# Attention in small steps for one more batch element, and Newton steps dealt out between products

## The chip, the cores and the metric

The kernel runs on one core of one Trainium2 chip. The metric is device time in microseconds (us). Before the change the median of three runs is 1347.16 us (1345.57 to 1347.76).

## The reference

Attention with RMS-normalised queries and keys, then one mixer layer over tokens and channels, in fp32 for q, k, v and with float64 weights:

```python
# q, k, v: (8, 12, 448, 64)
q_n, k_n = rmsnorm(q, g_q), rmsnorm(k, g_k)
attn = softmax(q_n @ k_n.T / sqrt(64))
x = (attn @ v).transpose(0, 2, 1, 3).reshape(8, 448, 768)
# token mixing: w_tok1 (448, 256), w_tok2 (256, 448)
u = x + (relu(x.T @ w_tok1) @ w_tok2).T
# channel mixing: w_ch1 (768, 1536), w_ch2 (1536, 768)
out = u + relu(u @ w_ch1) @ w_ch2
```

## The kernel before

**Work and its order.** The eight batch elements pass one after the other through the mixer. While element b is in the mixer, the attention of batch b + 1 is computed (AHEAD = 1) between the mixer's products. TensorE, VectorE, ScalarE and GpSimd run their instructions in the order in which the code issues them; only SyncE's DMA queue is ordered by the framework's scheduler.

**Attention.** Two heads are a pair, six pairs (NPAIR) a batch. Two pairs (four heads) are one t, so t runs from 0 to 23, three per batch. The 448 keys of a t are seven key blocks k of 64. `score(t, k)` makes 4 matmuls of 64x64 tiles into two s_ps tiles and two exponentials into an e tile; `values` multiplies e with v into o_ps; `group_sums` adds the e tiles of a t into es (k = 1, 2 on POOL, the rest on DVE); `row_sums` multiplies es by ones into d_ps. `denominators` for two pairs are two parts begin (a transpose and a reciprocal, which free d_ps) and two parts end (a transpose and a product, which free o_ps). There are four s_ps tiles (shared with d_ps), two o_ps and two m_ps tiles (for the mixer's products), four e tiles, and from t = BIG on a fifth e tile in cv_sb.

**Preparing the next t.** While t is computed, its successor's pairs n and n + 1 are prepared: `loads` (eight DMAs a pair from batch 2 on, into one of two qk_t slots), `square` on ACT, `reduce` on DVE, `roots`, `scale` on DVE, `turn_qk` (transposes). `roots` is a fold (four ACT copies, L1282), a guess (DVE, L1291 and L1296) and three Newton steps of three DVE instructions each (L1315 to L1317) on 128x56 elements.

**Small steps and large blocks.** Up to batch 1, attention comes in small steps, `att_step(g)` with g = 4t + s: four steps a t, with one or two key blocks of scores and of values each. Their items carry costs, and `merge` mixes them with the mixer's items in proportion to cost. From t = BIG on there are two large blocks a t (`big_step`): the first holds scores 0, 1 and 2 and the last values and row sums of t - 1; the second holds scores 3 to 6 and values 0 to 3. `place` puts six blocks per element ahead of the channel products number 0, 6, 11, 17, 22 and 28 (BLOCKS). A block's list `ahead` goes before it, `beside` directly behind it, and `between` is dealt out evenly over the products up to the next block.

**The mixer.** Token products (`tok1`, `tok2`, L754 and L762), then channel products in a seven-product form: 21 for `ch1` (L878), 21 for `ch2` (L935), each of 128x224 matmuls with weights from 384 KB unit loads, evicted by DVE (hb L883 and others), ACT or POOL. Element 0 instead multiplies with the weights as they are converted (`first_stage`, L850), with the conversion on DVE and ACT at the same time; in element 1, POOL also makes the weight sums (raw L204, loaded and stored by DMA, `sums`).

**Around the change.** In element 0 the attention list is the steps of batch 1 and, at its end, the first block of t = 6. In element 1, blocks 2 of t = 6 to 1 of t = 9 are placed. `cv_sb` serves the conversion in element 0.

Of the kernel before, what the change touches and what calls it, by code (L numbers as in the profile page):

```python
# [44 lines left out]
def whole(ctx, tc, shifted, pre, q, k, v, g_q, g_k, moe_w_tok1, moe_w_tok2, moe_w_ch1, moe_w_ch2, out):  # L45
# [6 lines left out]
    B, H, S, D = q.shape  # L52
# [6 lines left out]
    NPAIR = H // 2  # L59
# [50 lines left out]
    st = dict(pre.st)  # L110
# [262 lines left out]
    def e_tile(spare=False):  # L373

        if spare:
            return cv_sb[:].rearrange("p i n -> p (i n)")[:, 0:2 * S].rearrange("p (i s) -> p i s", i=2)
        return e_pool.tile([P, 2, S], F32, name="e")

    def score(t, k):

        e = st["e", t, k] = e_tile(t >= BIG and ((t - BIG) * NK + k) % 5 == 4)
        pss = [s_tile("s_ps") for i in range(2)]
        for i in range(2):
            qkT = st["qkT", 2 * t + i]
            for a in range(2):
                h = slice(a * D, a * D + D)
                nc.tensor.matmul(  # L387
                    out=pss[i][rows_of(i, a), 0:S], lhsT=qkT[h, 1, k * D:(k + 1) * D], rhs=qkT[h, 0, :],
                    start=True, stop=True)
        for i in range(2):  # L390
            nc.scalar.activation(out=e[:, i, :], in_=pss[i][:, 0:S], func=AF.Exp)  # L391
# [77 lines left out]
    def row_sums(t):  # L469
        es = st.pop(("es", t))  # L470
        for p in (2 * t, 2 * t + 1):
            st["d", p] = s_tile("d_ps")
            ones(p, es[:, p % 2, :], start=True, stop=True)

    def denominators(ps):

        def begin(p):
            b, j = divmod(p, NPAIR)
            if j == 0:
                st["uT", b] = uT_pool.tile([P, NC, S], F32, name="uT")  # L480
            ps = st.pop(("d", p))

            dt = rd_pool.tile([P, S], F32, name="dt", tag="rd")
            if shifted:
                nc.vector.tensor_scalar(dt[:], ps[:, 0:S], 1e-9, None, ALU.add)
                src = dt[:]
            else:

                src = ps[:, 0:S]
            nc.vector.transpose(out=dt[:], in_=src)  # L490
            st["rc", p] = rc = pre.nt_pool.tile([P, NB], F32, name="rc")
            nc.vector.reciprocal(out=rc[:], in_=dt[:].rearrange("p (n c) -> p n c", c=32)[:, :, 0])

        def raw(p):

            b, j = divmod(p, NPAIR)
            to = st["uT", b][:, j, :]
            nc.scalar.copy(out=to, in_=st["o", p][:, 0:S])
            st["o", p] = to

        def end(p):
            b, j = divmod(p, NPAIR)
            rd = rd_pool.tile([P, S], F32, name="rd", tag="rd")
            nc.vector.transpose(
                out=rd[:].rearrange("p (n c) -> p n c", c=32),
                in_=st.pop(("rc", p))[:].unsqueeze(2).to_broadcast([P, NB, 32]))
            nc.vector.tensor_tensor(out=st["uT", b][:, j, :], in0=st.pop(("o", p))[:, 0:S], in1=rd[:], op=ALU.mult)

        parts = [lambda p=p: begin(p) for p in ps]
        if ps[0] < NPAIR:  # L510
            parts += [lambda p=p: raw(p) for p in ps]
        return parts + [lambda p=p: end(p) for p in ps]

    NG = 2 * NP
    BIG = NPAIR

    def big_step(t, second):

        p, n = 2 * t, 2 * t + 2
        pair, last, live, more = (p, p + 1), (p - 2, p - 1), p < NP, 2 * t + 2 < NP  # L520
        item = lambda fn, *a, c=0.4: (c, lambda: fn(*a))
        loads = lambda j: [(0.3, fn) for fn in pre.loads(j, st, nc.sync, nc.sync)] if j < NP else []

        def first_block():
            if live:
                score(t, 0)
                score(t, 1)
            if more:
                pre.reduce(n, st)
                pre.square(n + 1, st)  # L530
            for k in range(NK - 2 - (t > BIG), NK):
                values(last, k)
            row_sums(t - 1)
            for i in last:
                st.pop(("v", i))
            if live:
                score(t, 2)

        def second_block():
            score(t, 3)  # L540
            score(t, 4)
            for k in range(4):
                values(pair, k)
            score(t, 5)
            score(t, 6)
            for i in pair:
                st.pop(("qkT", i))

        if not second:
            ahead = [item(pre.square, n, st)] if more else []  # L550
            beside = [item(pre.reduce, n + 1, st)] + [(0.4, fn) for fn in pre.roots(n, st)] if more else []
            between = [(0.4, fn) for fn in denominators(last)]
            between += [item(load_v, i, c=0.0) for i in pair if live]
            between += [item(group_sums, t, k) for k in (1, 2) if live]
            return ahead, (5.4, first_block), beside, between
        beside = [item(scale, n), item(scale, n + 1), item(turn_qk, n, 1), item(turn_qk, n, 0)] if more else []
        beside += [item(group_sums, t, k) for k in (3, 4)]
        between = [item(turn_qk, n + 1, 1), item(turn_qk, n + 1, 0)] + loads(n + 2) if more else []
        between += [item(group_sums, t, k) for k in (5, 6)] + loads(n + 3)
        return [], (6.2, second_block), beside, between  # L560
# [20 lines left out]
    def att_step(g):  # L581
# [101 lines left out]
        if not inside:  # L683
            items += part(turns)
        if g == 4 * BIG - 1 and not shifted:
            items += part(pre.loads(n + 3, st, nc.sync, nc.sync), 0.3)
# [294 lines left out]
    def y_order(b):  # L981

        return [o * KC + m for m in ((0, 1, 2) if b else (2, 0, 1)) for o in range(2)]

    def sends(b, cs):
        return [(0.3, lambda cc=cc: send_y(b, cc, st.pop(("y", cc)))) for cc in cs]
# [3 lines left out]
    def x_items(b, h):  # L990
        return [(0.1, lambda j=j: trans_x(b, j)) for j in range(h * NC // 2, (h + 1) * NC // 2)]

    def tok1_items(b, h):
        return [(us(NS, HC), lambda j=j, h=h: tok1(b, j, h)) for j in range(NJ)]
# [15 lines left out]
    def in_next(b):  # L1010


        return b < B - 1 and not shifted
# [36 lines left out]
    AHEAD = 1  # L1050
# [35 lines left out]
    per = NPAIR * 2  # L1086
# [8 lines left out]
    att_items = lambda lo, hi: [it for g in range(lo, hi) for it in att_step(g)]  # L1095
# [4 lines left out]
    for b in range(B):  # L1100
        early, double = middle_items(b)
        if b == 0:
            early, last = first_items(
                tok1_items(0, 0) + x_items(0, 1) + tok1_items(0, 1) + early, double, some)
        else:
            if b > 1 and in_next(b - 1):

                y, z = sends(b - 1, y_order(b - 1)[:4]), left
                left = [y[0], y[1], z[0], y[2], z[1], y[3]]
            run(merge(tok1_items(b, 0), left[:2]))  # L1110
            begin, early = merge(tok1_items(b, 1) + early[:3 * KC], left[2:]), early[3 * KC:]
            if b == 1:
                early, double = merge(begin + early, sums[5:20]), merge(double, sums[20:])
                begin = []
            early = begin + early + double
            early, last = early[:-4], early[-4:]
        lo = (b + AHEAD) * per + 1
        att = []
        if b + AHEAD < B and (shifted or not b):
            att = att_items(lo, lo + 10) + x_items(b + AHEAD, 0) + att_items(lo + 10, lo + per - (b == 0 and not shifted))  # L1120
            if not shifted:
                ahead, block, beside, between = big_step(BIG, False)
                att += ahead + [block] + beside + between
        elif b + AHEAD < B:
            t = (b + AHEAD) * NPAIR // 2
            blocks = [big_step(t + i // 2, i % 2) for i in range(1, NPAIR + 1)]
            blocks[4][3].extend(x_items(b + 1, 0))
            early = place(early, blocks, [near(early, at) for at in BLOCKS])
        if b == 0:
            last = x_items(1, 1) + merge(last, direct + sums[:5], turns(b, y_order(b)[2:4]))  # L1130
        else:
            if b + 1 < B:
                last = merge(last, x_items(b + 1, 1))
            last += last_items(b)
        run(merge(att, early) + last)
        if b == 0:
            load_units(0)
        left = turns(b, y_order(b)[4:])
# [187 lines left out]
def kernel(  # L1326
# [33 lines left out]
    with arm.Else():  # L1360
        whole(tc, True, pre, *args)
# [30 lines left out]
```

## Time and profile before

| | |
|---|---|
| median of 3 runs | 1347.16 us |
| the profiled execution, own time | 1349.28 us |
| its span (first to last instruction) | 1347.5 us |
| PE busy | 1276.4 us (95%) |
| DVE, POOL, ACT busy | 748.0, 383.1, 370.5 us |
| mean granted TensorE clock | 0.982 |
| element 1, from its first token product to the next one's | 176.4 us |
| elements 2 to 5, the same | 153.6 to 153.8 us each |

Everything in the profile is one execution. A line of the timeline gives the start, the length, the engine, the code line, the operation, the tile written and those read, shapes, how many instructions, and in brackets the idle time of that engine before it with what ended it. The window rows give busy time by engine, the granted clock and DMA's share for a stretch of the span.

### The profile page before, as it was taken

How to read it: one execution, taken by the hardware profiler on the slowest of the kernel's cores; microseconds unless marked ns; L12 is line 12 of the kernel's file. 1: busy time of each engine (PE TensorE's matmuls, PEld its weight loads, DVE VectorE, ACT ScalarE, POOL GpSimd, SP SyncE). 2: the span in 40 equal slices, each digit the busy share in tenths (PEclk: the TensorE clock that was granted, in tenths of full speed). 3: DMA queues.
4: the chain of work that ended last, by engine and by line, in shares of the span. 5: the costliest groups of instructions: out<-in, count | busy, mean ns of one | idle time of the engine just before them, and what ended most of it. 6: DMA issues, size and time to landing. Idle time of an engine off the chain costs nothing.

```text
span 1347.5 us, 20173 instructions
## 1 busy us (share of the span) xinstructions
PE 1276.4 (95%) x7408; PEld 937.7 (70%) x7408; DVE 748.0 (56%) x1289; ACT 370.5 (27%) x740; POOL 383.1 (28%) x449
## 2 busy tenths in 40 slices
PE   5989998899699999999999999999999999999997
PEld 3444444346578867786787867786777967797996
DVE  6887759824565256654566356654566456433212
ACT  5553423302332033311333033311343023300100
POOL 1211522164465123321223123322223213311220
PEclk9999998889899999999999999999999999999998
DMA  9655477789778867585766866585766954486554
GB/s 211 164 161 158 120 179 210 179 201 252 208 213 193 209 136 177 139 224 107 173 153 154 218 136 149 138 221 122 174 150 149 231 122 129 120 210 139 177 172 93
DMA packets 502448, 228.05 MB, mean 169 GB/s; under 512 B 374532, under 2 KB 464004, under 8 KB 502340
## 3 DMA queue, kind: packets, MB, share of 16 engines
q1 hardware_dynamic: 489218, 224.83, 67.7%
q10 hardware_dynamic: 12994, 1.84, 0.8%
q8 instruction: 61, 1.00, 0.3%
q14 instruction: 47, 0.39, 0.1%
q0 software_dynamic: 128, 0.00, 0.0%
HBM read 187.07 MB, written 39.52 MB: 168 GB/s over the span
## 4 chain that ended last, share of the span: by engine, by line
PE 69%; DVE 3%; DMA 3%; ACT 2%; POOL 1%; SPq 1%; issue 1%; ACTq 0%; DVEq 0%; POOLq 0%
PE m_ps L935 25%; PE m_ps L878 20%; PE s_ps L387 7%; PE o_ps L461 7%; PE m_ps L754 5%; PE m_ps L762 5%; PE d_ps L441 1%; ACT half L1282 1%; DMA qk_t<-in_k_dram 1%; DVE nt L1316 1%; DVE nt L1315 1%; DVE rs L1317 1%; DVE hb L908 0%; DMA ws<-raw 0%; ACT e L391 0%
## 5 line engine op out<-in xcount | busy, mean ns | idle before, releaser
L935 PEld LDWEIGHTS m_ps<-hb,unit 128*128 128x128 f32 x1764 | 332.5, 190 | 8.7 <-issue 8.5
L935 PE MATMUL m_ps<-hb,unit 128*128 128x224 f32 x1764 | 338.0, 353 | 0.0
L878 PE MATMUL m_ps<-tu,unit 128*128 128x224 f32 x1008 | 201.4, 354 | 0.0
L878 PEld LDWEIGHTS m_ps<-tu,unit 128*128 128x128 f32 x1008 | 189.2, 190 | 13.0 <-issue 5.6
L391 ACT ACTIVATE e<-s_ps 128x448 f32<-128x448 f32 x286 | 134.5, 549 | 213.5 <-PE s_ps L387 213.5
L878 PE MATMUL m_ps<-uT,unit 128*128 128x224 f32 x756 | 156.5, 361 | 23.7 <-DVE hb L883 19.1
L878 PEld LDWEIGHTS m_ps<-uT,unit 128*128 128x128 f32 x756 | 144.6, 194 | 32.8 <-DVE hb L883 21.2
L387 PE MATMUL s_ps<-qkT 64*64 64x448 f32 x1260 | 145.3, 548 | 4.2 <-ACT x L734 4.1
L461 PE MATMUL o_ps<-e,v 64*64 64x448 f32 x1116 | 129.2, 545 | 0.1
L944 POOL TENSOR_TENSOR uT<-uT,r 128x448 f32<-128x448 f32 (+1 forms) x56 | 49.6, 896 | 236.6 <-DVE r L944 151.1
L883 DVE TENSOR_TENSOR r<-m_ps,r 128x448 f32<-128x448 f32 x63 | 39.3, 623 | 111.9 <-PE m_ps L878 58.5
L944 DVE TENSOR_TENSOR uT<-uT,m_ps 128x448 f32<-128x448 f32 (+1 forms) x70 | 34.0, 502 | 119.6 <-PE m_ps L935 119.6
L387 PEld LDWEIGHTS s_ps<-qkT 64*64 64x64 f32 x1260 | 45.9, 133 | 72.9 <-issue 58.5
L429 DVE TENSOR_TENSOR es<-es,e 128x896 f32<-128x896 f32 x70 | 83.3, 1190 | 21.1 <-POOL es L429 16.5
L883 POOL TENSOR_TENSOR hb<-r,r 128x448 f32<-128x448 f32 x21 | 23.8, 1133 | 245.7 <-ACT r L899 236.6
L754 PE MATMUL m_ps<-x,w_sb 112*128 112x384 f32 x256 | 87.5, 500 | 4.2 <-DMA x<-xs 3.2
L461 PEld LDWEIGHTS o_ps<-e,v 64*64 64x64 f32 x1116 | 45.6, 135 | 62.3 <-issue 59.0
L1274 DVE TENSOR_REDUCE ms<-sq 128x28 f32<-128x896 f32 (+2 forms) x45 | 48.7, 1083 | 52.6 <-ACT sq L1260 50.0
L884 ACT ACTIVATE hb<-hb 128x448 f32<-128x448 f32 x63 | 36.3, 577 | 148.8 <-DVE hb L883 128.2
L754 PEld LDWEIGHTS m_ps<-x,w_sb 112*128 112x128 f32 x256 | 49.6, 195 | 39.6 <-issue 7.8
L762 PE MATMUL m_ps<-w_sb,h 128*128 128x448 f32 x192 | 74.7, 543 | 0.0
L767 DVE TENSOR_TENSOR uT<-uT,m_ps 128x448 f32<-128x448 f32 x48 | 29.4, 614 | 65.3 <-PE m_ps L762 65.3
(124 smaller groups left out, 1438.9 us busy)
## 6 DMA issues: line engine op xcount, KB each, us to landing
unit<-ws SPq DMA_DIRECT2D x294, 384.0 KB, 3.9
raw<-in_moe_w_ch_dram SPq DMA_DIRECT2D x72, 256.0 KB, 3.5
v<-in_v_dram SPq DMA_DIRECT2D x96, 112.0 KB, 3.7
xs<-xt SPq DMA_DIRECT2D x56, 168.0 KB, 4.3
x<-xs SPq DMA_DIRECT2D x14, 672.0 KB, 6.5
out_dram<-turned SPq DMA_DIRECT2D x168, 56.0 KB, 1.9
qk_t<-in_q_dram SPq DMA_DIRECT2D x144, 56.0 KB, 3.4
qk_t<-in_k_dram SPq DMA_DIRECT2D x144, 56.0 KB, 3.7
```

The lines of the kernel that those rows point to most:

```text
L387: nc.tensor.matmul(out=pss[i][rows_of(i, a), 0:S], lhsT=qkT[h, 1, k * D:(k + 1) * D], rhs=qkT[h, 0, :], start=True, stop=True)
L391: nc.scalar.activation(out=e[:, i, :], in_=pss[i][:, 0:S], func=AF.Exp)
L429: eng.tensor_tensor(out=es[:], in0=(es if k > 1 else st["e", t, 0])[:], in1=st["e", t, k][:], op=ALU.add)
L461: nc.tensor.matmul(out=st["o", p][a * D:(a + 1) * D, 0:S], lhsT=vt[rows, k * D:(k + 1) * D], rhs=e[rows, :], **kw)
L754: nc.tensor.matmul(out=ps[:, 0:HC], lhsT=w1_sb[0:R, c, jc * P:(jc + 1) * P], rhs=st["x", b, h][0:R, :, c, :], start=(c == 0), stop=(c == N ...
L762: nc.tensor.matmul(out=ps[:, 0:S], lhsT=st["h1", jc][:, cc * P:(cc + 1) * P], rhs=w2_sb[:, jc].rearrange("p c r -> p (c r)"), start=(jc == ...
L878: nc.tensor.matmul(out=ps[:, j * HS:(j + 1) * HS], lhsT=w[:, t, j, :], rhs=m, start=(t == 0), stop=(t == KC - 1))
L883: add = lambda e, o, x, y: e.tensor_tensor(out=o, in0=x, in1=y, op=ALU.add)
L884: relu = lambda x: nc.scalar.activation(out=x, in_=x, func=AF.Relu)
L935: nc.tensor.matmul(out=ps[:, j * HS:(j + 1) * HS], lhsT=st["w"](j, t), rhs=hb[:, HB[what], t, :], start=(t == 0), stop=(t == KF - 1))
L944: add = lambda e, o, x, y: e.tensor_tensor(out=o, in0=x, in1=y, op=ALU.add)
L1274: self.nc.vector.tensor_reduce(out=st["ms", p][:, p % 2, lo:hi], in_=sq[:, lo:hi], axis=AX_X, op=ALU.add)
```

## The change

BIG becomes NPAIR + NPAIR // 2 = 9 instead of 6. So the attention of batch 2 comes in small steps too: the last item in element 0 is step g = 24 (scores 0 of t = 6) instead of a first block, and element 1 merges steps 25 to 35 and then the first block of t = 9 with its mixer items, from the second half of the first token product on. Elements 2 to 6 place their blocks as before. The fifth e tile is used from t = 9 on.

In every first block's lists, `roots` leaves `beside` and goes to `between`. The order of `between` becomes: the group sums 1 and 2, the fold, both begins, the guess, then end, Newton step, end, Newton step, the last Newton step, and the two loads of v.

```diff
-    BIG = NPAIR
+    BIG = NPAIR + NPAIR // 2
...
         if not second:
             ahead = [item(pre.square, n, st)] if more else []
-            beside = [item(pre.reduce, n + 1, st)] + [(0.4, fn) for fn in pre.roots(n, st)] if more else []
-            between = [(0.4, fn) for fn in denominators(last)]
-            between += [item(load_v, i, c=0.0) for i in pair if live]
-            between += [item(group_sums, t, k) for k in (1, 2) if live]
+            beside = [item(pre.reduce, n + 1, st)] if more else []
+            between = [item(group_sums, t, k) for k in (1, 2) if live]
+            ends, roots = ([(0.4, fn) for fn in fns] for fns in (denominators(last), pre.roots(n, st) if more else []))
+            between += roots[:1] + ends[:2] + roots[1:2]
+            between += [it for both in zip(ends[2:], roots[2:4]) for it in both] if more else ends[2:]
+            between += roots[4:] + [item(load_v, i, c=0.0) for i in pair if live]
             return ahead, (5.4, first_block), beside, between
...
-        if b + AHEAD < B and (shifted or not b):
-            att = att_items(lo, lo + 10) + x_items(b + AHEAD, 0) + att_items(lo + 10, lo + per - (b == 0 and not shifted))
-            if not shifted:
+        if b + AHEAD < B and (shifted or b < 2):
+            att = att_items(lo, lo + 10) + x_items(b + AHEAD, 0) + att_items(lo + 10, lo + per - (b == 1 and not shifted))
+            if b and not shifted:
                 ahead, block, beside, between = big_step(BIG, False)
                 att += ahead + [block] + beside + between
```

## The prediction

> **What bounds the kernel now.** I read the page first. PE is busy for 95% of the span and its row of slices is nearly solid, so only PE's idle time and its slow stretches can be taken out; the clock row dips in the first third alone.
>
> ```profile
> PE 1276.4 (95%) x7408; PEld 937.7 (70%) x7408; DVE 748.0 (56%) x1289; ACT 370.5 (27%) x740; POOL 383.1 (28%) x449
> PEclk9999998889899999999999999999999999999998
> ```
>
> Next the busy time by stages. The cuts are the times at which an element's first token product (L754) starts; the columns are window, length, then busy us of PE, PEld, DVE, ACT, POOL, then clock, DMA share and GB/s.
>
> ```profile
> 127.00:284.60 157.60, 147.98 (x580) 69.09 (x573) 116.10 (x189) 49.67 (x94) 53.54 (x78) 0.96 0.68 171
> 284.60:461.00 176.40, 160.09 (x925) 123.84 (x924) 86.80 (x152) 42.49 (x88) 82.23 (x122) 0.94 0.87 224
> 614.80:768.60 153.80, 151.44 (x922) 118.44 (x921) 85.86 (x152) 42.25 (x87) 40.87 (x32) 1.00 0.69 162
> ```
>
> The rows are element 0 (with the attention of batch 1), element 1 (with batch 2) and element 3, which stands for elements 2 to 6. Element 1 does the same PE work as element 3 and takes 22.6 us more, with DMA at 0.87 and a clock of 0.94. Element 3 is idle for 2.4 us only.
>
> Third, the timeline of PE and then of DVE behind a first block of element 3.
>
> ```profile
> 658.52 2.43 PE L878 MATMUL m_ps<-uT,unit 128*128 128x224 f32 x12
> 662.67 2.54 PE L878 MATMUL m_ps<-uT,unit 128*128 128x224 f32 x12 [1.72 <-DVE hb L883]
> ```
> ```profile
> 655.09 1.09 DVE L1274 TENSOR_REDUCE ms<-sq 128x28 f32<-128x896 f32 x1 [2.03 <-ACT sq L1260]
> 658.31 0.22 DVE L1291 SCALAR_TENSOR_TENSOR ms<-ms,half 128x56 f32<-128x56 f32 x1 [2.14 <-ACT half L1282]
> ...
> 660.79 0.22 DVE L1317 SCALAR_TENSOR_TENSOR rs<-nt,rs 128x56 f32<-128x56 f32 x1
> 660.93 1.15 DVE L908 SCALAR_TENSOR_TENSOR hb<-r,hb 128x448 f32<-128x448 f32 x2
> 662.00 0.62 DVE L883 TENSOR_TENSOR hb<-m_ps,r 128x448 f32<-128x448 f32 x1
> ```
>
> DVE ends the second square sum at 656.2, stands 2.1 us for ACT's fold, works 2.7 us on the guess and three Newton steps, and only then evicts the product that PE ended at about 658.6. With two m_ps tiles, the next product but one waits for that. The same idle times recur in elements 2 to 6: 2.69, 2.36, 2.35, 2.37 and 1.71, **11.5 us** in all.
>
> Fourth, element 1: PE, then ACT, then DVE; and the two idle times at the ends of element 0.
>
> ```profile
> 349.72 4.73 PE L878 MATMUL m_ps<-uT,unit 128*128 128x224 f32 x12 [10.19 <-DVE hb L883]
> 391.22 4.22 PE L878 MATMUL m_ps<-uT,unit 128*128 128x224 f32 x12 [2.08 <-DVE r L883]
> ```
> ```profile
> 342.24 0.95 ACT L1260 ACTIVATE sq<-qk_t 128x896 f32<-128x896 f32 x1 [8.47 <-DMA ws<-raw]
> ```
> ```profile
> 343.22 1.08 DVE L1274 TENSOR_REDUCE ms<-sq 128x28 f32<-128x896 f32 x1 [10.06 <-ACT sq L1260]
> ```
> ```profile
> 250.96 2.19 PE L441 MATMUL d_ps<-es,one_c 64*64 64x448 f32 x8 [4.83 <-ACT e L391]
> 290.54 8.19 PE L754 MATMUL m_ps<-x,w_sb 112*128 112x384 f32 x16 [3.18 <-DMA x<-xs]
> ```
> ```profile
> POOL raw L204 <- DMA raw<-ws: 20.3, 2, 11.0
> ```
>
> ACT waits to square pair 17, whose eight loads SP issues between 329.2 and 338.8, among weight transfers. DVE stands for the square, the eviction stands behind DVE, PE behind the eviction. At 250.96 it is the same kind: the square of pair 14 stands in ACT's queue ahead of the exponentials and itself waits 4.84 us for its loads. At 290.54 PE waits for the second half of x with nothing else to do.
>
> **What the Trainium skill says.** "TensorE: Matmul & The Clock Gate", Part 1, has PE at half rate after an idle window of about 3.4 us. The trace agrees: the windows 340 to 350 and 350 to 360 show clocks of 0.70 and 0.79, so some 10 us at half rate, which costs 2.2 us of work beyond the 10.19 us gap. The same page, under the array's architectural detail, calls ACT and DVE strict FIFO; the rows above are that queue. "DMA: Bandwidth & Descriptors", Specifications, asks for at least 512 B per packet for line rate; here 374,532 of 502,448 packets are smaller, the q and k loads among them, and DMA is the crowded resource of element 1.
>
> **The change part by part.**
>
> *Elements 2 to 6, Newton between products.* Beside a first block only the square sum is left. The fold, the guess and the Newton steps (2.7 us of DVE, 1.0 us of ACT) are dealt out over the five following products with the four denominator parts; the group sums on POOL come first. DVE can then evict the product behind the block at about 658.7 instead of 662.0, so the gap goes. What is late next: per product of 2.3 us, DVE gets two begins and the guess (2.2 us), then an end and a Newton step (2.0), then an end and two steps (2.8), beside 0.6 for the eviction. At the worst place it is 1.5 us behind, under the 2.3 us that two m_ps tiles allow, and a second block of 6 us without m_ps follows. The ends free o_ps before that block's values; the roots are due at scale, after it. POOL is idle there (10.3 us before 661.7), so its two sums of 2.1 us cost nothing. The v loads move last: their tiles are free from the first block on, they land in 3.7 us (median), and 11 us of products cover them; without that cover a value product would wait up to about 3 us. Value: −11.5 + 1.0 left over = **−10.5**; bounds −11.5 and 0.
>
> *Element 1, small steps.* Gone or covered: the 10.2 gap and its 2.2 of slow clock; 2.1 at 391 with 1.7 of clock; 0.9 before row sums at 332; and 3.2 at 290 with 2.9 of clock (0.69 from 290 to 300), because the step with scores 1 and 2 now stands between the two halves of the token product. That is 23.2. Pair 17 in particular: laying out the merge by its costs, its loads can start after the second channel product and its square comes after the seventh, with two attention steps between, about 18 us. Now there are about 11. The loads took about 20 from their first chance to landing, so a few us of waiting stay. Paid: six more switches between products and attention at 0.2 (a second block takes 6.17 for eight key blocks of 0.747), 1.1; two score key blocks that element 0 did, 1.5; DVE in the token phase, where two scalings, four transposes and four group sums (about 12 us) fall on 20 us of products with their own evictions, 3; pair 17, 3; waits of the other pairs, 2. Sum −23.2 + 10.6 = **−12.6**; bounds −20.6 (no new wait) and above zero (below).
>
> *Element 0.* The block in its last quarter becomes a step without a square ahead of the exponentials: −4.8 and −2.1 of clock at 251, −1.5 of moved scores, + 2.0 for the square of pair 14, which still waits for loads somewhere behind = **−6.4**. The attention list becomes shorter, and the other steps slide by a product. The 4.6 gap at 208 (an eviction on ACT behind a square) may go, with 3 us of slow clock, or another may come; I take 0, bounds −7.6 and +5.
>
> The packets moved are the same; eight loads of pair 15 start later in element 0 and are needed in element 1 only. SP's queue keeps its kinds of work. POOL's group sums of batch 2 now stand among the weight sums.
>
> Sum: −10.5 − 12.6 − 6.4 = −29.5. The profiled execution took 1349.28 (span 1347.5 and 1.8 around it), 2.1 above the median 1347.16. So 1319.8 by its count, and **1318** by the median's.
>
> **The rivals.**
>
> *Element 1 is bound by its transfers.* Then late loads only move to another place, and it saves the wait for x alone: −6.1 + 2.6 + 2.0. For it: a DMA share of 0.87 over the stage, and of 1.06 and 1.17 in the two 10 us windows ahead of the gap (320 to 340). Against: it falls to 0.77 from 340 to 350, and the square comes 7 us later. −1.5 − 10.5 − 6.4 gives **1329**.
>
> *The Newton work shifts the gap.* DVE does as much per product and the gap appears two products on. Against: the 2.1 us stand for the fold vanishes from DVE. Without the 10.5 it is **1328**.
>
> *Element 1 gets worse: POOL's queue.* In small steps the group sums of keys 1 and 2 stand on both sides of a weight sum on POOL, which waits 11.0 and 9.3 us for raw (20.3 above); DVE's group sum for key 3 follows from POOL's, and the evictions of the token products stand behind it. There are four e tiles instead of five. If both waits reach PE, that is 20.3 + 2 × 2.2 of clock; if two odd pairs are as late as pair 17 now, 24.8 more: 49.5 against 23.2 − 2.6 + 10.5 + 1.5 = 32.6, so +17, **1364**. It decides from 33 us of new idle time in element 1. Against: the raw load concerned was issued at 291 and lands about when the first step is over, and the long second wait begins after those sums.
>
> *The change hardly acts*, as the sums cancel: 1347.
>
> **How the numbers follow.** Likeliest case 0.60; transfers 0.20; shifted gap 0.07; POOL 0.09; cancelled 0.04. The likeliest case's own bounds reach from about 1305 to 1330; the range up to 1342 takes in the two milder rivals with a part of element 1's unknown waits. About 0.2% (2.7 us) is what a measurement here can tell from no change. Faster 0.87, same 0.04, slower 0.09.
>
> **What would show it.** Right: element 3 at about 151.5 us with no PE idle time ended by DVE hb L883 behind a block; element 1 near 164; no wait of DVE for sq of 10 us; the clock row without its dip near 344; the token product at 290 without a wait for x. Wrong: PE waits in elements 2 to 6 of over 1 us, or DVE es waiting for POOL es in the token phase of element 1.

## The result, and the profile after

The changed kernel takes **1331.65 us** (median of 4 runs, 1330.89 to 1332.47) against 1346.75 us of the kernel before in the same session (4 runs): a ratio of 0.9888, with a 95% interval of 0.9871 to 0.9905. It is faster, by about half of what was forecast. The profiled execution took 1331.61 us with a span of 1329.6, so 17.9 us less span than before. The lines of kernel.py have moved by two behind the edited lists: L878 is now L880, L935 is L937.

The page after, its rows of busy time and of the granted clock:

```profile
PE 1272.4 (96%) x7408; PEld 936.3 (70%) x7408; DVE 767.0 (58%) x1289; ACT 372.0 (28%) x740; POOL 381.0 (29%) x449
PEclk9999999899998999999999999999999999999999
```

The stages after, cut where an element's first token product starts: elements 0, 1, 3 and 6 (window, length, busy us of PE, PEld, DVE, ACT, POOL, then clock, DMA share, GB/s):

```profile
86.30:274.40 188.10, 177.31 (x748) 84.14 (x749) 147.04 (x224) 63.53 (x117) 58.94 (x90) 0.96 0.68 174
274.40:448.40 174.00, 161.09 (x938) 120.68 (x937) 97.31 (x163) 45.94 (x97) 90.00 (x124) 0.95 0.89 226
600.40:752.50 152.10, 151.06 (x922) 118.86 (x922) 88.78 (x152) 42.44 (x87) 39.20 (x32) 1.00 0.69 164
1056.70:1205.20 148.50, 148.50 (x898) 117.67 (x897) 71.72 (x120) 33.13 (x67) 35.08 (x30) 1.00 0.62 152
```

And before, cut at the same events (elements 0, 1 and 3):

```profile
86.10:282.00 195.90, 182.20 (x764) 86.04 (x765) 150.48 (x236) 66.49 (x126) 62.50 (x92) 0.96 0.65 166
282.00:457.20 175.20, 158.89 (x921) 123.07 (x920) 86.42 (x151) 42.53 (x88) 82.23 (x122) 0.94 0.87 222
611.20:764.80 153.60, 151.24 (x921) 118.25 (x920) 86.23 (x152) 42.25 (x87) 40.87 (x32) 1.00 0.69 161
```

The table and the prediction cut the profile of before 2.6 to 3.8 us behind these starts, and element 0 even 41 us behind (127 instead of 86.1), so their 176.4 us for element 1 is 175.2 here. Element 0 lost 7.9 us, elements 2 to 6 lost 8.6 together (1.9, 1.6, 1.6, 1.5, 2.0), and element 1, where most was expected, only **1.2**.

Behind a first block of element 3, the timeline of PE and of DVE after the change:

```profile
645.37 2.54 PE L880 MATMUL m_ps<-tu,unit 128*128 128x224 f32 x12
647.74 4.70 PE L880 MATMUL m_ps<-uT,unit 128*128 128x224 f32 x24
```
```profile
644.79 1.15 DVE L910 SCALAR_TENSOR_TENSOR hb<-r,hb 128x448 f32<-128x448 f32 x2
647.94 0.62 DVE L885 TENSOR_TENSOR hb<-m_ps,r 128x448 f32<-128x448 f32 x1 [2.00 <-PE m_ps L880]
```

PE runs through: 24 matmul records in one piece where the kernel before had its 1.72 us. DVE now waits for PE at that eviction, not PE for DVE. The waits named in the prediction (1.7 to 2.1 and 0.6 per element) are gone, but a new one stands behind the third first block of elements 2 to 5. In element 1 all the old waits are gone too, and two new ones have come. The two of element 1 and the first of the four others:

```profile
298.39 1.86 PE L764 MATMUL m_ps<-w_sb,h 128*128 128x448 f32 x2 [4.52 <-DVE uT L769]
414.46 2.19 PE L441 MATMUL d_ps<-es,one_c 64*64 64x448 f32 x8 [8.23 <-ACT e L391]
579.91 4.40 PE L937 MATMUL m_ps<-hb,unit 128*128 128x224 f32 x22 [1.04 <-issue]
```

### The profile page after: what moved, and what is told of

The parts are those of the page before. It is cut to its first block, busy times and chain, and to the rows that moved or that the text cites. A ratio compares the mean times of both kernels' runs of the same rounds, so it can differ in the third digit from the quotient of the medians.

```text
span 1329.6 us, 20169 instructions
## 1 busy us (share of the span) xinstructions
PE 1272.4 (96%) x7408; PEld 936.3 (70%) x7408; DVE 767.0 (58%) x1289; ACT 372.0 (28%) x740; POOL 381.0 (29%) x449
## 4 chain that ended last, share of the span: by engine, by line
PE 82%; DVE 8%; DMA 4%; issue 2%; POOL 1%; SPq 1%; ACT 1%; DVEq 0%; POOLq 0%; ACTq 0%
PE m_ps L880 25%; PE m_ps L937 25%; PE s_ps L387 9%; PE o_ps L461 8%; PE m_ps L764 5%; PE m_ps L756 5%; PE m_ps L852 2%; DMA raw<-in_moe_w_ch_dram 1%; PE d_ps L441 1%; DVE raw L264 1%; DVE raw L281 1%; DVE stage L308 1%; DVE cv_sb L263 1%; PE t_ps L361 1%; DVE ms L1276 1%
## 5 line engine op out<-in xcount | busy, mean ns | idle before, releaser
L937 PE MATMUL m_ps<-hb,unit 128*128 128x224 f32 x1764 | 339.9, 354 | 4.2 <-issue 4.2
L937 PEld LDWEIGHTS m_ps<-hb,unit 128*128 128x128 f32 x1764 | 332.8, 190 | 15.7 <-issue 10.1
L880 PE MATMUL m_ps<-tu,unit 128*128 128x224 f32 x1008 | 201.6, 355 | 0.0
L880 PEld LDWEIGHTS m_ps<-tu,unit 128*128 128x128 f32 x1008 | 189.1, 190 | 14.1 <-issue 7.8
L391 ACT ACTIVATE e<-s_ps 128x448 f32<-128x448 f32 x294 | 138.5, 549 | 175.6 <-PE s_ps L387 173.7
L880 PE MATMUL m_ps<-uT,unit 128*128 128x224 f32 x756 | 150.7, 353 | 0.0
L880 PEld LDWEIGHTS m_ps<-uT,unit 128*128 128x128 f32 x756 | 142.6, 190 | 5.0 <-issue 4.3
L756 PE MATMUL m_ps<-x,w_sb 112*128 112x384 f32 x256 | 84.8, 488 | 1.0 <-ACT x L736 1.0
L764 PE MATMUL m_ps<-w_sb,h 128*128 128x448 f32 x192 | 78.0, 559 | 4.5 <-DVE uT L769 4.5
L764 PEld LDWEIGHTS m_ps<-w_sb,h 128*128 128x128 f32 x192 | 36.6, 196 | 42.4 <-issue 27.4
## 6 DMA issues: line engine op xcount, KB each, us to landing
xs<-xt SPq DMA_DIRECT2D x56, 168.0 KB, 4.5
```

What stands on the lines that cost most here:

```text
L756: nc.tensor.matmul(out=ps[:, 0:HC], lhsT=w1_sb[0:R, c, jc * P:(jc + 1) * P], rhs=st["x", b, h][0:R, :, c, :], start=(c == 0), stop=(c == N ...
L764: nc.tensor.matmul(out=ps[:, 0:S], lhsT=st["h1", jc][:, cc * P:(cc + 1) * P], rhs=w2_sb[:, jc].rearrange("p c r -> p (c r)"), start=(jc == ...
L880: nc.tensor.matmul(out=ps[:, j * HS:(j + 1) * HS], lhsT=w[:, t, j, :], rhs=m, start=(t == 0), stop=(t == KC - 1))
L937: nc.tensor.matmul(out=ps[:, j * HS:(j + 1) * HS], lhsT=st["w"](j, t), rhs=hb[:, HB[what], t, :], start=(t == 0), stop=(t == KF - 1))
```

## The experiments

Each was run against the kernel before on the same chip, in four sessions in which the kernel before took 1347.68 to 1350.43 us; the times are medians. e1 to e4 are one session, e5, e6, e8 and e9 the second, e10 to e12 the third, e13 the fourth, so across sessions the ratios and the element lengths compare better than the times. "Element" lengths come from the one profiled execution, cut as above.

### The two parts apart

e1 keeps `BIG = NPAIR` and the old condition in the loop and has only the new lists; e2 has only the other part:

```diff
 e1, against the kernel before (the rest of the new lists as in the change)
-            beside = [item(pre.reduce, n + 1, st)] + [(0.4, fn) for fn in pre.roots(n, st)] if more else []
+            beside = [item(pre.reduce, n + 1, st)] if more else []
 e2, against the kernel before (the rest of the loop as in the change)
-    BIG = NPAIR
+    BIG = NPAIR + NPAIR // 2
```

> The new lists of the first blocks with BIG left at 6. If the two parts work in different places: elements 2 to 6 fall by 1.6 to 2.0 us each (8.6 together, as in the changed kernel), element 1 loses the 2.1 us wait near 391 and its 1.7 us of slow clock but keeps the 10 us wait for pair 17, element 0 is as before: about 1334 us. If the gain of elements 2 to 6 needs the later BIG (other e tiles, other positions), it is 1343 or more.

> BIG at 9 with the old lists of the first blocks. If the parts work in different places: element 0 falls by about 8 us, element 1 by about 1, elements 2 to 6 stay at 153.7: about 1338 us. If the small steps cost more than they save, and the changed kernel's gain is the Newton part's alone: 1346 or more.

e1 took 1345.15 us against 1348.51 (ratio 0.9978, 0.9960 to 0.9996), e2 1338.79 (0.9933, 0.9908 to 0.9957). In spans: e1 0.7 us less than before, e2 10.2, both together 17.9. e2 is as expected: elements 2 to 6 stay (element 3 at 153.7), element 0 falls by 8.5, element 1 by 0.7. e1 has the 1.6 us in each of elements 3 to 5, 7.0 in elements 2 to 6, but its element 1 grew from 175.2 to 181.8 us. The profiled execution is one of e1's longer ones (1348.65 us; its twelve runs go from 1341.56 to 1350.50): by the medians e1 gains 3.4 us where elements 2 to 6 alone give 7.0, so by estimate they lose 3.6 in element 1 (7.0 less 3.4), not 6.6, with an interval of about 2.4 either way. So the parts seem to depend on each other: dealt out among the large blocks of element 1, the new lists cost something, and moving the blocks out of that element avoids it. The sum doesn't show it clear of the noise: the medians of the two parts add up to 13.1 of the 15.1 us. One of e1's waits there, in PE's timeline:

```profile
362.33 3.08 PE L461 MATMUL o_ps<-e,v 64*64 64x448 f32 x10 [4.06 <-DMA v<-in_v_dram]
```

The loads of v, last in the new list, come late where DMA is full. e9 is e1 with them first:

```diff
-    between = [item(group_sums, t, k) for k in (1, 2) if live]
+    between = [item(load_v, i, c=0.0) for i in pair if live] + [item(group_sums, t, k) for k in (1, 2) if live]
...
-    between += roots[4:] + [item(load_v, i, c=0.0) for i in pair if live]
+    between += roots[4:]
```

> As e1 (BIG at 6, Newton steps dealt out), but the two loads of v stand first in the list instead of last. If their late place cost e1 its 4.1 us wait of the values for v near 362 and the slow clock behind it: element 1 falls from 181.8 to about 176 and the time from 1345 to about 1339 us. If v comes late because DMA is full whatever its place: as e1, 1345.

e9 took 1351.85 us (ratio 1.0030, 1.0016 to 1.0045): slower than before. The wait for v is gone, but element 1 is as long as in e1 (182.1), with a weight load late at its end, and elements 3 to 5 are 1.1 longer than in e1, because the ends are now dealt later and the second block waits for o_ps:

```profile
449.78 2.62 PE L937 MATMUL m_ps<-hb,unit 128*128 128x224 f32 x9 [3.78 <-DMA unit<-ws]
560.26 2.11 PE L461 MATMUL o_ps<-e,v 64*64 64x448 f32 x20 [1.39 <-DVE uT L507]
```

So v's place is one of the costs of e1 and not all of it. What else lengthens element 1 there (the wait for x is 1.9 us longer than before, a block near 406 waits 2.7 us) was not taken apart.

### The 1.04 us in elements 2 to 5

Both kernels differ from the changed one in the lists alone. e4 gives the last first block of an element its old lists; e6 puts the group sums at the end:

```diff
 e4
+    if t % 3 or t == BIG:
         (the new lists)
+    else:
+        (the old lists)
 e6
-    between = [item(group_sums, t, k) for k in (1, 2) if live]
...
     between += roots[4:] + [item(load_v, i, c=0.0) for i in pair if live]
+    between += [item(group_sums, t, k) for k in (1, 2) if live]
```

> The changed kernel, but the first blocks of t = 12, 15, 18 and 21 (the last block of an element, with three products behind it) have the old lists. If the 1.04 us wait of elements 2 to 5 is an eviction on DVE behind thirteen items dealt over three products: it goes in each, about 1327.5 us. If it is a weight load that comes late, as the row's word 'issue' says: it stays, 1331.5; if the old lists cost something there: above that.

> The changed kernel with POOL's two group sums behind a first block moved from the front of the list to its end; the Newton steps stay dealt out. If the 1.04 us wait of elements 2 to 5 comes from DVE's small instructions running slowly (guess and Newton at 1 to 2 us instead of 0.2) while POOL makes the group sums beside them: they fall to 0.2 and the wait goes, about 1327 us. If it comes from too many items over three products alone: it stays near 1 us and the time near 1331.

e4 took 1325.92 us (ratio 0.9836, 0.9812 to 0.9860), and its elements 3 to 5 fell from 152.07 to 150.8 us, with no PE wait of 0.05 us or more left in elements 2 to 6:

```profile
599.30:750.10 150.80, 150.80 (x921) 118.98 (x921) 86.04 (x152) 42.52 (x87) 39.28 (x32) 1.00 0.69 166
```

So the wait was DVE's, not a weight load's. Behind the third block three products remain, and thirteen items come five, four and four; DVE in the changed kernel, then POOL in the same stretch:

```profile
571.98 0.85 DVE L1293 SCALAR_TENSOR_TENSOR ms<-ms,half 128x56 f32<-128x56 f32 x1
572.87 1.98 DVE L1298 TENSOR_SCALAR rs<-ms 128x56 int32<-128x56 int32 x1
...
575.97 1.06 DVE L1317 SCALAR_TENSOR_TENSOR nt<-rs 128x56 f32<-128x56 f32 x1
577.07 0.22 DVE L1318 TENSOR_TENSOR nt<-nt,ms 128x56 f32<-128x56 f32 x1
```
```profile
572.72 2.07 POOL L429 TENSOR_TENSOR es<-e 128x896 f32<-128x896 f32 x1
574.87 2.09 POOL L429 TENSOR_TENSOR es<-es,e 128x896 f32<-128x896 f32 x1
```

The guess takes 0.85 and 1.98 us beside POOL's work and 0.22 and 0.19 without it. With the Newton instruction at 575.97, three instructions took 3.9 us instead of 0.6. An estimate from these lines: without those 3.3 us, DVE's next eviction (from 578.67) would have come early enough to spare PE its 1.04 us. In the old lists those small instructions run before the sums. e4 changes the dealing and this overlap together, so it doesn't say which of the two makes the wait.

e6 was a miss for both theories: 1348.45 us (ratio 0.9994, 0.9982 to 1.0005), the whole gain lost. Elements 2 to 4 took 156.5 us. POOL still made its sums in the same stretch (from 573.7), since it was free whatever the place in the list, and the guess ran as slowly as before (0.85 and 1.98 us), so e6 doesn't separate the two theories either. But the sums at the front had cost DVE nothing and taken the first two places; without them each DVE item came up to one product sooner, ahead of an eviction:

```profile
503.43 1.78 PE L880 MATMUL m_ps<-tu,unit 128*128 128x224 f32 x8 [1.11 <-DVE hb L885]
```
```profile
582.30 1.92 PE L937 MATMUL m_ps<-hb,unit 128*128 128x224 f32 x5 [2.41 <-issue]
```

Here the order of the new list is worth at least as much as the dealing out: elements 2 to 5 stand at 152.1 us with the sums first, 154.8 to 156.5 with them last, 153.7 to 154.0 before.

### The 8.2 us in element 1

ACT in the changed kernel, at the first block of t = 9:

```profile
413.03 0.95 ACT L1262 ACTIVATE sq<-qk_t 128x896 f32<-128x896 f32 x1 [12.06 <-DMA qk_t<-in_q_dram]
413.88 1.83 ACT L391 ACTIVATE e<-s_ps 128x448 f32<-128x448 f32 x4
```

The square of pair 20 is `ahead` of the block, its loads are not there, and the exponentials stand behind it; row sums wait for their s_ps tiles. It is of the same kind as the 4.8 us wait that element 0 had before the change, in the place to which the block has moved; e2, with the old lists, has it there too (9.2 us). e3 takes the squares and sums out of that block; e12 (on top of e4) issues the loads sooner:

```diff
 e3
-            if more:
+            if more and t > BIG:
                 pre.reduce(n, st)
                 pre.square(n + 1, st)
...
-            ahead = [item(pre.square, n, st)] if more else []
+            ahead = [item(pre.square, n, st)] if more and t > BIG else []
...
+            if t == BIG:
+                beside = []
+                between = [item(group_sums, t, k) for k in (1, 2)] + ends
+                between += [item(pre.square, n, st), item(pre.reduce, n, st)]
+                between += [item(pre.square, n + 1, st), item(pre.reduce, n + 1, st)]
+                between += roots + [item(load_v, i, c=0.0) for i in pair]
 e12
     att = att_items(lo, lo + 10)
+    if b == 1 and not shifted:
+        att += [(0.6, fn) for fn in pre.loads(20, st, nc.sync, nc.sync)]
     att += x_items(b + AHEAD, 0) + att_items(lo + 10, ...)
...
-        elif live and s == 3 and not pre.plain(n):
+        elif live and s == 3 and not pre.plain(n) and (shifted or n != 18):
```

> The changed kernel, but in the first block of t = 9 the squares of pairs 20 and 21 and their sums no longer stand ahead of or inside the block; they follow the group sums and the denominators. If the 8.2 us wait near 414 is exponentials standing behind a square that waits for its loads: that wait and 2.5 us of slow clock go, 1 to 3 us come back where evictions stand behind the same square: about 1323 us. If PE then waits as long at the next eviction, since the loads come no sooner: about 1331.

> e4, with the loads of pair 20 ahead of the stores and loads of x for element 2 in the order of issue. If the square of pair 20 waits since its loads queue behind the x stores: the 8.2 us wait near 414 shrinks by 4 us or more and 1 to 2 us of slow clock with it, about 1321 us. If DMA is full there and other transfers take the place: 1326.

> e4 and e3 together: the old lists for the last first block of elements 2 to 5, and the squares behind the first block of t = 9 in element 1. If the two act in different places, the sum: e4's time less the 2.6 us that e3 took from element 1, about 1323 us. If the end of element 1 is bound by weight loads whatever PE waits for: as e4, 1326.

e3 took 1328.08 us (ratio 0.9855, 0.9830 to 0.9881). The wait and its slow clock went, but element 1 fell by 2.6 us only (174.0 to 171.4). e10 (e3 and e4 together) took 1323.52 us (0.9804, 0.9773 to 0.9834), 2.4 below e4, with element 1 as in e3 (171.4) and elements 3 to 5 as in e4 (150.8): the two edits add. Where e3's gain goes is seen in e10's PE timeline:

```profile
414.32 3.67 PE L949 MATMUL m_ps<-hb,unit 128*128 128x224 f32 x18 [0.97 <-DMA unit<-ws]
...
427.17 4.81 PE L949 MATMUL m_ps<-hb,unit 128*128 128x224 f32 x24 [2.97 <-DVE uT L958]
434.02 2.32 PE L949 MATMUL m_ps<-hb,unit 128*128 128x224 f32 x11 [2.04 <-DMA unit<-ws]
```

A PE that doesn't stand meets weight loads that are late, and an eviction behind the sum of the late pair. e12 took 1320.38 us (0.9787, 0.9757 to 0.9817), 5.5 below e4, from element 1 (174.0 to 168.7): the square of pair 20 no longer waits, and 4.0 us are left at pair 21. ACT and then PE in e12:

```profile
398.42 0.93 ACT L1271 ACTIVATE sq<-qk_t 128x896 f32<-128x896 f32 x1
400.98 1.85 ACT L391 ACTIVATE e<-s_ps 128x448 f32<-128x448 f32 x4 [1.62 <-PE s_ps L387]
414.72 0.95 ACT L1271 ACTIVATE sq<-qk_t 128x896 f32<-128x896 f32 x1 [11.88 <-DMA ws<-raw]
```
```profile
417.94 7.29 PE L943 MATMUL m_ps<-hb,unit 128*128 128x224 f32 x22 [4.02 <-issue]
```

The transfers are the same, only their order differs. In the changed kernel SP issues nothing from 386.3 to 394.1, then the stores of x, with pair 20's eight loads among and behind them from 396.2 to 407.6; in e12 it issues these loads from 389.5 to 393.9. So their place in the order of issue made pair 20 late. e12 moves them ahead of the last attention step of t = 8 as well as of x, and doesn't show which of the two counts.

> e12 with e10's edit as well: old lists for the last first block, loads of pair 20 ahead of the x transfers, squares of pairs 20 and 21 behind the first block of t = 9. If the 4.0 us wait that e12 keeps near 418 is an eviction behind the sum of pair 21: it goes, and the time is about 1317 us. If weight loads are late there, as in e3 and e10: 1320 or more.

e13 has all three edits: 1319.80 us (0.9779, 0.9750 to 0.9808), not measurably below e12; its element 1 is at 168.0. The 4.0 us went, and 2.8 and 1.7 came a few us later, the first behind DVE and the second for a weight load. It has the lowest time of the kernels here, by ratio 2.2% below the kernel before.

### The 4.5 us in the token phase of element 1

DVE stands there from 263 on for POOL and then has the sum and the Newton steps of t = 7's first pair ahead of the evictions; in the changed kernel, DVE and then POOL:

```profile
287.05 0.65 DVE L973 STREAM_TRANSPOSE turned<-uT 128x448 f32<-128x448 f32 x1 [23.80 <-POOL uT L862]
...
290.83 1.16 DVE L1293 SCALAR_TENSOR_TENSOR ms<-ms,half 128x56 f32<-128x56 f32 x1 [1.08 <-ACT half L1284]
...
293.80 1.99 DVE L1317 SCALAR_TENSOR_TENSOR nt<-rs 128x56 f32<-128x56 f32 x1
...
297.73 1.14 DVE L769 TENSOR_TENSOR uT<-uT,m_ps 128x448 f32<-128x448 f32 x2
```
```profile
282.35 0.45 POOL L204 TENSOR_TENSOR raw<-raw 128x128 f32<-128x128 f32 x1 [12.58 <-DMA raw<-ws]
...
293.65 2.07 POOL L429 TENSOR_TENSOR es<-es,e 128x896 f32<-128x896 f32 x1
```

The guess and the Newton steps fall on POOL's work and take 7.0 us (290.83 to 297.81), where the prediction's lines show 2.7.

e5 moves the square, the sum and the roots one step later; e11 (on top of e4) leaves two instead of five weight-sum items at the end of element 0:

```diff
 e5
-    behind = (a, b + pre.roots(n, st), scales(n), [])[s]
+    roots = b + pre.roots(n, st)
+    behind = (a, roots, scales(n), [])[s] if t > 6 else (a, [], roots + scales(n), [])[s]
 e11
-    last = x_items(1, 1) + merge(last, direct + sums[:5], ...)
+    last = x_items(1, 1) + merge(last, direct + sums[:2], ...)
...
-    early, double = merge(begin + early, sums[5:20]), ...
+    early, double = merge(begin + early, sums[2:20]), ...
```

> The changed kernel, but in element 1 the square and sum of pair 15 and the roots of t = 7's first pair stand behind the second attention step instead of the first. If the 4.5 us wait of the token products near 298 comes from DVE, which starts these items late (it waits for POOL) and has them ahead of the evictions: wait and 2.5 us of slow clock go, 1 to 2 us come back, about 1326 us. If DVE has too much to do in the token phase wherever they stand: 1330 to 1333.

> e4, with POOL's first three weight sums made in element 1's token phase instead of at the end of element 0 (the loads for them are issued at the old place for two, later for the others). If the 4.5 us wait of the token products near 298 begins with POOL standing 12 us for the first raw weights, with its residual sums of element 0 and then DVE's transposes behind it: DVE is free before the tokens, the wait and its 2.5 us of slow clock go: about 1320 us. If the weight sums then come late for the channel products, or POOL stands as long a little later: 1326 or more.

e5 took 1331.43 us (ratio 0.9880): no change, the wait is 4.1 us at the same place, since now DVE's group sums wait for POOL's and stand ahead of the eviction. In e11 DVE no longer stands for POOL beyond 276.8 (288.8 in the changed kernel), and the token wait falls to under 0.5 us. But that is not the chain of the expectation at work. DVE comes to the eviction 23.2 us after the start of the element, as in the changed kernel (23.3); PE comes some 4 us later than there, because it has waited for x. PE and then DVE in e11:

```profile
281.76 2.52 PE L762 MATMUL m_ps<-x,w_sb 112*128 112x384 f32 x5 [2.28 <-DMA x<-xs]
```
```profile
297.39 1.14 DVE L775 TENSOR_TENSOR uT<-uT,m_ps 128x448 f32<-128x448 f32 x2
```

So the cause of the 4.5 us is read from the trace and not shown by an experiment: DVE starts late behind POOL, and then is slow beside it. An estimate from these lines gives the second more weight: the late start costs at most 2.4 us (ACT's square ends at 286.3, DVE's sum of it begins at 288.7), the slow instructions 4.3 (7.0 less 2.7). e11 took 1328.65 us (0.9839, 0.9809 to 0.9870), by ratio level with e4; its element 1 is 177.5 us instead of 174.0, with waits for x (2.3 us near 282), for scores near 360 (1.6) and the 8.8 us at the block of t = 9. Why the element ends later by so much was not settled.

### The step at the end of element 0

e8 puts an empty item of cost 2.4 ahead of element 0's last attention step:

```diff
-            att = ... + att_items(lo + 10, lo + per - (b == 1 and not shifted))
+            att = ... + att_items(lo + 10, lo + 11)
+            att += [(2.4, lambda: None)] * (b == 0) + att_items(lo + 11, lo + per - (b == 1 and not shifted))
```

> The changed kernel with an empty item of cost 2.4 ahead of the last attention step of element 0, which so falls one product later. If the 4.8 us wait near 240 is a score whose transposes stand on DVE behind the weight conversion: the wait goes with 2.7 us of slow clock, about 1325 us. If the wait goes along with the step: 1331.

e8 took 1337.27 us (ratio 0.9914, 0.9889 to 0.9938), by ratio 0.3% above the changed kernel; its element 0 is 194.0 us instead of 188.1. The item moves the proportions of the whole merge, and with them every step of element 0 by up to a product. So neither theory is tested cleanly. The wait near 240 fell to 2.0 us, one of 3.4 us came near 260, and the old one near 208 was back, as PE's timeline shows:

```profile
208.49 4.07 PE L852 MATMUL m_ps<-hb,stage 128*128 128x448 f32 x5 [4.49 <-ACT hb L864]
```

## Why the prediction was right or wrong

The direction and the range held (1331.65 in 1305 to 1342), the size did not: 29.5 us were forecast by the profiled execution's own count, 17.7 were measured there (1349.28 to 1331.61), and 15.1 by the medians, since that one execution of before lay 2.5 us above its session's median. Of the prediction's own signs, two spoke against it: DVE still waits 10.3 us for a square, at t = 9, and PE waits in elements 2 to 5 came to just over 1 us. A slip without consequence: the lower bounds of its parts (−11.5, −20.6, −6.4 and −7.6) lead to about 1301, not 1305.

*Elements 2 to 6* (−10.5, measured −8.6). The mechanism was right, point by point: DVE evicts at once, POOL's sums cost PE nothing, no value product of elements 2 to 6 waits for v. Mis-sized was what is left over: 1.0 for all elements, measured 1.04 in each of four. The working counted DVE's items over five products; behind the third block there are three, and beside POOL's sums the guess took 2.8 us instead of 0.4.

*Element 1* (−12.6, measured −1.2). This is the step that failed. The 23.2 us of old waits all went, that of pair 17 too (3 were set aside for it, nothing was left). The failing term is "waits of the other pairs, 2": it was 8.2 us and 2.5 of slow clock at t = 9. The working took the block with a square ahead of its exponentials out of element 0 as a gain of 6.9, and didn't follow it to the place where it went. "DVE in the token phase, 3" was 4.5 and 2.5 of slow clock. With the 2.6 for switches and scores as priced, that makes −2.9; 1.7 us more were not traced. The rival that element 1 is bound by transfers was half right: e3 met late weight loads, yet e12 shows 5.3 us to be had from their order.

*Element 0* (−6.4, measured −7.9). The wait at 251 went as priced. The one at 208, taken at 0 with a bound of −7.6, went as well, and a new wait of 4.84 us at 240 with 2.7 of slow clock took its place: by the trace, the transposes of pair 13 stand on DVE behind the weight conversion. e8 shows that both move with the place where the merge puts the steps. So the sum was near by luck: one term left out took away what another, also left out, gave.

*POOL's queue*, the rival for slower: its path exists (e5's trace shows it), and it cost at most the 7 us of the token phase, far below the 33 from which it would have decided. The prediction saw it in the wrong place: in the changed kernel the Newton steps stood behind POOL and ran slowly beside it, not the group sums.

The sum closes: against −29.5, element 1 brought 11.4 less, elements 2 to 6 1.9 less, element 0 1.5 more, the tail and the start 0.2 more: −17.9.

## What to carry to other kernels

When work moves from one stage to another, price the waits that it carries with it at the new place: a square ahead of a block in ACT's queue waits for its loads in whatever stage the block stands. Where many small items are dealt out between evictions, the order counts as much as the dealing: items that cost the evicting engine nothing belong at the front, and the shortest stretch (here three products) sets the wait. Before small DVE instructions are moved, look at what POOL does beside them: the same guess and Newton steps took 2.7 us in one place and 7.0 in another. A gap that is closed shows the next limit; here that was weight loads, and the order of the DMA issues moved 5 us where moving the waiting instruction moved 2.6.

## What the runs showed of the hardware

DVE's small instructions slow down while POOL works. In elements 2 to 6 of the changed kernel the first instruction of the guess takes 0.15 us where no POOL instruction overlaps it, and up to 1.1 where one does; the second 0.19 and 1.0 to 2.0; the first of a Newton step 0.21 and 0.8 to 1.1. The transposes and the product from PSUM beside them kept their 0.6 us. Their end goes with the end of POOL's instruction: of the guess and Newton instructions on 128x56 elements, 51 in the changed kernel and 580 in all fourteen traces took over 0.3 us, and every one of them ended 0.04 to 0.08 us behind the end of a POOL instruction, the longest (2.0 to 2.1 us) beside POOL's group sums of 2.1 us. The Trainium skill, "GPSIMD Engine Reference", Specifications, says that POOL shares its SBUF interfaces with DVE, with contention for instructions of two SBUF inputs or a two-port mode; the trace agrees.

Ahead of the last one, at the end of the span, the slow clock came in stretches of 3.4, 6.8 or 10.2 us. Behind the first 60 us of the span, in all fourteen traces, each PE wait of 3.05 us or more had such a stretch beside it, and no wait from 1.0 to 2.0 us had one. Of the thirteen waits from 2.0 to 3.0 us seven had one (2.08, 2.28, 2.31, 2.66 and three of 2.41 to 2.42) and six not (2.04, 2.05, 2.45, 2.81, 2.96, 2.97). So the idle window of about 3.4 us in the Trainium skill, "TensorE: Matmul & The Clock Gate", Part 1, is not a floor for a wait here: a wait of 2.1 us can be followed by the slow clock too.
